# Two double PSUM banks for row maxima and three single banks, in the steps with little filler work

## The chip, the cores and the metric

The kernel runs on one core of one Trainium2 chip. The metric is the device time of one execution in microseconds (us), lower is better. A core has a matrix engine (TensorE, PE in the profile), a vector engine (VectorE, DVE), a scalar engine for functions (ScalarE, ACT), a programmable engine (GpSimd, POOL) and a queue engine for DMAs (SyncE, SP). Matmul results land in PSUM, which has eight banks of 512 fp32 numbers for each of the 128 partitions.

## The reference

Two layers, each an attention block with 16 query heads that share one key and one value head, and a gated feed-forward block; both add to the residual.

```python
def _A_ref(x, wq, wk, wv, wo):
    B, S, D = x.shape          # 1, 2048, 448
    H = 16                     # Dh = 28
    q = (x @ wq).reshape(B, S, H, Dh).transpose(0, 2, 1, 3)
    k = x @ wk
    v = x @ wv
    scores = jnp.einsum("bhqd,bkd->bhqk", q, k) * (Dh ** -0.5)
    p = _softmax(scores, axis=-1)
    o = jnp.einsum("bhqk,bkd->bhqd", p, v)
    return o.transpose(0, 2, 1, 3).reshape(B, S, H * Dh) @ wo

def _B_ref(x, w_gate, w_up, w_down):            # F = 1792
    h = _sigmoid(x @ w_gate) * (x @ w_up)
    return h @ w_down

x = x + _A_ref(_layernorm(x), A_wq, A_wk, A_wv, A_wo)
x = x + _B_ref(_layernorm(x), B_w_gate, B_w_up, B_w_down)
# and both once more, with the same weights
```

## The kernel before

Weights and activations are split into two fp16 parts (high and low), and products are sums of several fp16 matmuls. Queries are worked on in 16 tiles u of 128 rows, keys in 16 tiles kt of 128. The heads form four groups g of four heads each; a group of scores is one matmul of 512 columns.

The main loop (the body of the function behind the start-up) runs over **steps**, one for each (u, kt), 256 in a layer. A step computes:

- four **scores** tiles (`scores`, matmul at L566): keys against the four heads of a group, 128 x 512 in PSUM, named `s`; ScalarE turns each into P = exp(...) in SBUF (L570);
- **PV** (`pv`, L584): four groups of P times the values, added up over the 16 key tiles in one PSUM bank of its own, named `pv`, from pool `psv`;
- two half groups of **maxima** for the next query tile (`mx_gen`, matmul at L509): queries against 512 keys, for two heads at a time, into two PSUM tiles named `mx`; VectorE takes the maximum of each over its 512 columns (L512). They are needed before the scores of that query tile, since the maximum is subtracted inside the score matmul: `maxima` reduces them, transposes them on TensorE (`mt`) and a DMA puts them into the query tile QS;
- **filler** work from `Filler`: generators that give out one matmul at a time, of the query projections of this layer (`qproj`, tile `qp`, 11 matmuls), of the output projection (`wo`, 12 matmuls), and of the feed-forward block (`gp`, `up`, `dn`, matmuls at L369 and L789). `fill.slice` gives out as many as a budget allows (`debt`); `rate` is what is left over the steps that are left.

The order inside two steps is one of two strings, letter by letter: S is a scores tile, M a whole group of maxima (four tiles), m half of one (two tiles), P a PV, T the transposes of finished maxima, F a slice of filler, X the bookkeeping of a step (with stages of the block behind the attention, and in layer 0 pieces of weight preparation, `paced`). `FULL` is used when `rate` is over `LEANR` = 600 and `LEAN` otherwise, which is so at the beginning of each layer, while no feed-forward block is ready:

```python
FULL = "FSFSFSFSTPPXMFSFSFSFSFXM"
LEAN = "FSFSFSFSmPTXmFSFSFSFSmPTXm"
```

At the key tiles of `MORE` = (5, 10) of a layer's first query tile, an additional whole group of maxima is issued.

All engines run their own instructions in order. A PSUM tile is taken from a pool when it is written first and goes back when its last reader is done; the next tile that gets its bank waits for that reader by a semaphore. All tiles but `pv` share one pool `psf` with seven banks, whatever their kind:

```python
BANKS = {"s": "f", "m": "f"}
NBK = {"f": 7, "s": 2, "m": 3}
psf = ctx.enter_context(tc.tile_pool(name="psf", bufs=1, space=PSUM))
```

What reads a PSUM tile is often put off with `defer` and issued at the next `flush`, which a slice of filler begins with.

Of the kernel before, what the change touches and what calls it, by code (L numbers as in the profile page):

```python
# [19 lines left out]
def interleaved_layers_kernel(ctx: ExitStack, tc: tile.TileContext, x, wq, wk, wv, wo, wg, wu, wd, out, layers=2):  # L20
# [27 lines left out]
    psv = ctx.enter_context(tc.tile_pool(name="psv", bufs=1, space=PSUM))  # L48
    BANKS = {"s": "f", "m": "f"}
    NBK = {"f": 7, "s": 2, "m": 3}  # L50
    psf = ctx.enter_context(tc.tile_pool(name="psf", bufs=1, space=PSUM))

# [43 lines left out]
    def fps(shape, dt, name):  # L96
        flush()
        return psf.tile(shape, dt, tag="f", name=name, bufs=NBK["f"])

# [289 lines left out]
    def kv_t(l, XT, t, kt):  # L389
        p = fps([128, 160], F32, "kv")  # L390
        X = lambda c, k: XT[:k, c, t * 128:(t + 1) * 128]
        yield from chain(p[:, 0:128], lambda a, c, k: WKV[:k, a, c, Dh:], X, 64, True)
        yield from chain(p[:, 128:156], lambda a, c, k: WKV[:k, a, c, 0:Dh], X, 40, False)
        c = slice(kt * 128, (kt + 1) * 128)

        def build():
            nc.scalar.activation(KK[l][:, 1, c], p[:, 0:128], AF.Identity, scale=ek, bias=row)
            nc.scalar.activation(VV[l][:, kt, 0:28], p[:, 128:156], AF.Copy, scale=2.0 ** -16)
            nc.vector.scalar_tensor_tensor(KK[l][64:96, 0, c], p[64:96, 0:128], ek[64:96], KK[l][64:96, 1, c],
                                           op0=OP.mult, op1=OP.subtract)  # L400
            nc.gpsimd.tensor_copy(KK[l][0:64, 0, c], KK[l][0:64, 1, c])
        defer(build)

    def kv(l, XT, t, kt):
# [3 lines left out]

        def build():
            nc.scalar.activation(kt_[:, :, 0:28], p[:, None, 28:56].to_broadcast([128, 8, 28]), AF.Copy, scale=ek)  # L410
            nc.scalar.activation(VV[l][:, kt, 0:28], p[:, 0:28], AF.Copy, scale=2.0 ** -16)
# [9 lines left out]
    def qproj(l, XT, b, g):  # L421
# [4 lines left out]

        def ev():
            q = wk1.tile([128, 2, 512], F16, name="qst")
            hi = QH0[:, g] if l + b == 0 else q[:, 0]
# [62 lines left out]
    def mx_gen(l):  # L492
# [3 lines left out]
        for u in range(U):  # L496
# [3 lines left out]
            for kb in range(NB):  # L500
                ks = slice(kb * 512, (kb + 1) * 512 - 128 * (few and kb == NB - 1))
                nk = ks.stop - ks.start
                for g in range(G):
                    assert KVD[l] >= ks.stop // 128
                    for hh in (0, 2):
                        ps = {h: psf.tile([128, 512], F32, tag=BANKS["m"], name="mx", bufs=NBK[BANKS["m"]])
                              for h in (hh, hh + 1)}
                        for h in ps:
                            nc.tensor.matmul(ps[h][:, :nk], qh[32 * h:32 * h + 32, g], KK[l][32 * h:32 * h + 32, 1, ks],  # L509
                                             start=True, stop=True, tile_position=(32 * h, 0))  # L510
                        for h in ps:
                            nc.vector.tensor_reduce(mp[:, g, h, kb:kb + 1], ps[h][:, :nk], axis=AX.X, op=OP.max)  # L512
                        ps = None
                        if hh == 0:
# [8 lines left out]
            if few:  # L523
                assert KVD[l] == KT
                for hh in (0, 2):
                    ps = {h: psf.tile([128, 4, 128], F32, tag=BANKS["m"], name="mx", bufs=NBK[BANKS["m"]])
                          for h in (hh, hh + 1)}
                    for g in range(G):
# [34 lines left out]
    def scores(l, u, kt, g, P):  # L563
        assert ("m", l, u) in stored, (l, u, kt)
        s = psf.tile([128, 512], F32, tag=BANKS["s"], name="s", bufs=NBK[BANKS["s"]])
        nc.tensor.matmul(s, KK[l][0:96, 0, kt * 128:(kt + 1) * 128], QS[l, u][:, g].rearrange("p h n -> p (h n)"),  # L566
# [59 lines left out]
    class Block:  # L626
# [8 lines left out]
        def tile(self, u):  # L635
# [56 lines left out]
            def wo():  # L692
# [7 lines left out]

                def f():
                    nc.vector.scalar_tensor_tensor(self.x1[:, t], p, osc, v["xr"], op0=OP.mult, op1=OP.add)
                    v["ls"] = ln_stats(self.x1[:, t])[0]
# [34 lines left out]
        def bulk(self):  # L738
# [3 lines left out]
            def glu(f):  # L742
# [8 lines left out]
                th = wk1.tile([128, 512], F32, tag="s2", name="th", bufs=3)  # L751
                defer(lambda: nc.scalar.activation(th, gp.rearrange("p j n -> p (j n)"), AF.Tanh, scale=gsc))  # L752
                up = fps([128, 2, TB * 128], F32, "up")
# [3 lines left out]

                def ev():
                    t = th
                    nc.vector.scalar_tensor_tensor(t, th, 1.0, up.rearrange("p j n -> p (j n)"), op0=OP.add, op1=OP.mult)  # L760
# [18 lines left out]
        def down(self, t, hs):  # L779
# [14 lines left out]

            def ev():
                x2 = v["x2"] = wk1.tile([128, D], F32, tag="xr", name="x2", bufs=4)
                nc.vector.scalar_tensor_tensor(x2, p, dsc, self.x1[:, t], op0=OP.mult, op1=OP.add)  # L797
# [43 lines left out]
    class Filler:  # L841
# [16 lines left out]
        def slice(self, ns):  # L858
# [18 lines left out]
            if not self.gens and not self.first:  # L877
                self.debt = min(self.debt, 0.0)

    fill = Filler()  # L880
    LOADS = [(4, 4), (8, 4), (12, 2), (14, 2)]
# [32 lines left out]
    def warmth(n):  # L914
        p = psf.tile([128, 128], F32, tag="f", name="sca", bufs=NBK["f"])
        for _ in range(n):
# [217 lines left out]
    for n in range(NPR):  # L1134
        task("A", 0.9, [], wprep, late=LP, at=PR0 + PRP * n)
    run_tasks(task("V", 0.1, prev[-1:], finish, late=-5.0))
    if not ro:
        load_ro()
# [15 lines left out]
    for l in range(layers):  # L1154
# [12 lines left out]
        if l == 0:  # L1167
            warmth(8)
        rate = 0.0
        PQ = []  # L1170
        step = 0
        P = []
        sn = 0
        while step < U * KT:
            order = FULL if rate > LEANR else LEAN
            for o in order:
                u, kt = divmod(step, KT)
# [83 lines left out]
```

## Time and profile before

| what | us |
| --- | --- |
| median of three runs | 2255.53 (2253.49 to 2256.1) |
| the profiled execution | 2254.95 |
| its span, first to last instruction | 2253.2 |
| ScalarE busy (L570 alone) | 1392.8 (1136.8) |
| POOL busy | 1047.2 |
| lean steps of layer 0, from their first exponential to the first of the step behind them | 107.67 to 265.42 |
| first 44 steps of layer 1, from their first score to the first of the step behind them | 1212.17 to 1349.32 |

The page of a profile lists for each engine its busy time, share of the span and number of instructions; then groups of instructions by source line, engine, operation and tiles (out<-in), with shapes, count, busy time and the mean of one in ns, and behind the second bar the idle time of the engine just before them and who ended it. The order-of-time view lists start, length, engine, line and tiles, merges equal neighbours (x4), and has in brackets the idle time ahead and its releaser. PE rows are matmuls and overlap: a matmul of 512 columns is shown with 0.38 us, though the next one starts 0.22 us behind it. The rows by window give, for a stretch, its length, the busy time and number of instructions of PE, PE's weight loads, DVE, ACT and POOL, then the granted clock, the DMA share and GB/s.

### The profile page before, as it was taken

The numbers are of one execution on the slowest core, as the hardware profiler recorded it, in microseconds if no ns is written. First come the engines' busy times: TensorE is split into PE (matmuls) and PEld (weight loads), VectorE is DVE, ScalarE is ACT, GpSimd is POOL, SyncE is SP. The second block draws the span as 40 slices with busy tenths as digits, with TensorE's granted clock in tenths as the row PEclk, the third lists the DMA queues.
The fourth block names the chain that finished last, engine by engine and source line by source line (L and its number), as shares of the span: only waits on it lengthen the run. The fifth ranks groups of instructions, "written<-read, shape, count | busy, mean of one in ns | idle before, by whom it ended". The sixth has DMA issues, their size and how long they took to land. (4 is left out here: it accounts for less than half of the span.)

```text
span 2253.2 us, 43077 instructions
## 1 busy us (share of the span) xinstructions
PE 2202.5 (98%) x16336; PEld 1059.4 (47%) x16336; DVE 1675.4 (74%) x2921; ACT 1392.8 (62%) x2567; POOL 1047.2 (46%) x1363
## 2 busy tenths in 40 slices
PE   8999999999999999999999999999999999999999
PEld 6322354544545444454573224545454544445457
DVE  7898887877778787774457988878787877878322
ACT  4676766666666666666424676666666666666641
POOL 4367551555455554546402014545545555454540
PEclk8999999999999999999999999999999999999999
DMA  5734642323313232332351113223132313233233
GB/s 150 214 104 134 189 157 61 94 76 103 109 57 105 66 90 80 98 96 79 102 143 57 34 47 107 81 85 101 60 94 65 102 57 102 80 95 89 76 103 122
DMA packets 224400, 217.53 MB, mean 97 GB/s; under 512 B 154048, under 2 KB 185536, under 8 KB 224192
## 3 DMA queue, kind: packets, MB, share of 16 engines
q1 hardware_dynamic: 217200, 198.89, 30.3%
q0 software_dynamic: 3680, 12.09, 1.5%
q10 hardware_dynamic: 3312, 3.79, 0.5%
q8 instruction: 128, 2.10, 0.4%
q14 instruction: 80, 0.66, 0.1%
HBM read 175.37 MB, written 23.59 MB: 88 GB/s over the span
## 5 line engine op out<-in xcount | busy, mean ns | idle before, releaser
L512 DVE TENSOR_REDUCE mp<-mx 128x1 f32<-128x512 f32 x2048 | 1268.0, 680 | 293.7 <-PE mx L509 288.2
L570 ACT ACTIVATE P<-s 128x512 f32<-128x512 f32 x2048 | 1136.8, 600 | 561.9 <-PE s L566 542.7
L566 PE MATMUL s<-QS,KK 96*128 96x512 f16 x2048 | 727.2, 380 | 17.6 <-DVE mp L512 8.3
L369 PEld LDWEIGHTS <-wgu 128*128 128x128 f16 x4928 | 460.4, 97 | 254.9 <-issue 91.8
L604 POOL TENSOR_TENSOR PH<-P,PH 128x512 f16<-128x512 f32 x384 | 459.1, 1195 | 30.8
L603 POOL CAST PH<-P 128x512 f16<-128x512 f32 x384 | 249.4, 649 | 466.6 <-ACT P L570 466.6
L584 PE MATMUL pv<-P,VV 128*32 128x512 f32 x3328 | 418.3, 599 | 0.0
L369 PE MATMUL gp<-XT,wgu 128*128 128x256 f16 x2464 | 387.4, 273 | 0.8 <-DVE mp L512 0.7
L369 PE MATMUL up<-XT,wgu 128*128 128x256 f16 x2464 | 385.7, 273 | 1.0 <-ACT P L570 0.4
L789 PE MATMUL dn<-WD,h 128*128 128x448 f16 x1344 | 330.4, 353 | 0.0
L509 PE MATMUL mx<-KK,QH 32*128 32x512 f16 x2048 | 261.8, 384 | 6.5 <-ACT P L570 3.1
L566 PEld LDWEIGHTS <-KK 96*128 96x128 f16 x2048 | 192.1, 97 | 132.3 <-issue 41.1
L509 PEld LDWEIGHTS <-QH 32*128 32x128 f16 x2048 | 63.8, 91 | 345.1 <-issue 343.1
L789 PEld LDWEIGHTS <-h 128*128 128x128 f16 x1344 | 124.7, 98 | 138.6 <-issue 23.7
L584 PEld LDWEIGHTS pv<-P,VV 128*32 128x32 f32 x3328 | 86.4, 109 | 155.5 <-issue 135.4
L764 DVE SCALAR_TENSOR_TENSOR h<-th,h 128x512 f16<-128x512 f32 x112 | 100.1, 894 | 48.4 <-ACT h L763 48.4
L763 ACT ACTIVATE h<-th 128x512 f16<-128x512 f32 x112 | 70.3, 628 | 87.1 <-DVE th L760 86.1
L760 DVE SCALAR_TENSOR_TENSOR th<-th,up 128x512 f32<-128x512 f32 x112 | 75.9, 678 | 57.3 <-PE up L369 51.8
L675 POOL TENSOR_TENSOR lb<-pvs,lb 128x512 f32<-128x512 f32 x32 | 40.7, 1273 | 141.1 <-DMA lb<-sums 99.3
L752 ACT ACTIVATE th<-gp,gsc 128x512 f32<-128x512 f32 x112 | 76.9, 686 | 44.5 <-PE gp L369 44.1
L369 PE MATMUL qp<-XT,WQ 128*128 128x512 f16 x352 | 100.2, 392 | 0.7 <-DVE ktl L412 0.7
L329 POOL TENSOR_SCALAR rs<-mv 128x1 f32<-128x1 f32 x48 | 11.0, 229 | 179.9 <-DVE mv L324 179.9
(164 smaller groups left out, 1106.9 us busy)
## 6 DMA issues: line engine op xcount, KB each, us to landing
wgu<-wgu_d SPq DMA_DIRECT2D x224, 512.0 KB
QS<-qd SPq DMA_DIRECT2D x384, 32.0 KB
lb<-sums SPq DMA_DIRECT2D x120, 64.0 KB
wgu_d<-sgu POOLq DMA_DIRECT2D x14, 512.0 KB, 3.6
qd<-qst POOLq DMA_DIRECT2D x16, 256.0 KB, 2.6
xr<-in_A_x_dram SPq DMA_DIRECT2D x16, 224.0 KB
QH<-qd SPq DMA_DIRECT2D x28, 128.0 KB
x2d<-x SPq DMA_DIRECT2D x16, 224.0 KB
```

The lines of the kernel that those rows point to most:

```text
L369: nc.tensor.matmul(ps, a, b, start=n == 0, stop=n == 10)
L509: nc.tensor.matmul(ps[h][:, :nk], qh[32 * h:32 * h + 32, g], KK[l][32 * h:32 * h + 32, 1, ks], start=True, stop=True, tile_position=(32 * ...
L512: nc.vector.tensor_reduce(mp[:, g, h, kb:kb + 1], ps[h][:, :nk], axis=AX.X, op=OP.max)
L566: nc.tensor.matmul(s, KK[l][0:96, 0, kt * 128:(kt + 1) * 128], QS[l, u][:, g].rearrange("p h n -> p (h n)"), start=True, stop=True)
L570: nc.scalar.activation(p, s, AF.Exp, scale=ESC)
L584: nc.tensor.matmul(v[32 * g:32 * g + 32], VV[l][:, kt], P[g], start=kt == 0, stop=kt == KT - 1, tile_position=(0, 32 * g))
L603: {"A": nc.scalar.copy, "V": nc.vector.tensor_copy, "P": nc.gpsimd.tensor_copy}[e](h[:, 0], p)
L604: nc.gpsimd.tensor_tensor(h[:, 1], p, h[:, 0], op=OP.subtract)
L752: defer(lambda: nc.scalar.activation(th, gp.rearrange("p j n -> p (j n)"), AF.Tanh, scale=gsc))
L760: nc.vector.scalar_tensor_tensor(t, th, 1.0, up.rearrange("p j n -> p (j n)"), op0=OP.add, op1=OP.mult)
L764: defer(lambda: nc.vector.scalar_tensor_tensor(h[:, 1], t, 2.0 ** -17, h[:, 0], op0=OP.mult, op1=OP.subtract), 1)
L789: nc.tensor.matmul(p, hs[f // 2][:, a, o:o + 128], WD[:, f, c], start=n == 0, stop=n == 3 * FC - 1)
```

## The change

The pool of the seven banks gets two layouts. In layout "F" it is as before. In layout "L" two double banks (tag `m2`, a tile of 2 x 512) belong to the maxima, and three single banks to everything else. A pair of maxima then is one tile, written by the same two matmuls and read by one VectorE instruction over 2 x 512 that gives two numbers a partition. `bank` replaces the direct calls of the pool, and counts the tiles of filler that are open in `live`; the instructions that read them count down (`freed`). Before the layout changes, `Filler.close` runs filler until none is open.

```diff
-    BANKS = {"s": "f", "m": "f"}
-    NBK = {"f": 7, "s": 2, "m": 3}
-    psf = ctx.enter_context(tc.tile_pool(name="psf", bufs=1, space=PSUM))
+    NBK = {"F": 7, "L": 3}
+    pools, psum, live = ctx.enter_context(ExitStack()), {}, [0]
...
+    def banks_as(mode):
+        pools.close()
+        psum["mode"] = mode
+        psum["pool"] = pools.enter_context(tc.tile_pool(name="psf", bufs=1, space=PSUM))
+
+    def bank(shape, dt, name):
+        live[0] += name in ("kv", "qp", "wo", "gp", "up", "dn")
+        return psum["pool"].tile(shape, dt, tag="f", name=name, bufs=NBK[psum["mode"]])
...
-                        ps = {h: psf.tile([128, 512], F32, tag=BANKS["m"], name="mx", bufs=NBK[BANKS["m"]])
-                              for h in (hh, hh + 1)}
+                        two = psum["mode"] == "L"
+                        if two:
+                            both = psum["pool"].tile([128, 2, 512], F32, tag="m2", name="mx", bufs=2)
+                            ps = {h: both[:, h - hh] for h in (hh, hh + 1)}
+                        else:
+                            ps = {h: bank([128, 512], F32, "mx") for h in (hh, hh + 1)}
...
-                        for h in ps:
-                            nc.vector.tensor_reduce(mp[:, g, h, kb:kb + 1], ps[h][:, :nk], axis=AX.X, op=OP.max)
-                        ps = None
+                        if two:
+                            nc.vector.tensor_reduce(mp[:, g, hh:hh + 2, kb:kb + 1], both[:, :, :nk], axis=AX.X, op=OP.max)
+                        else:
+                            for h in ps:
+                                nc.vector.tensor_reduce(mp[:, g, h, kb:kb + 1], ps[h][:, :nk], axis=AX.X, op=OP.max)
+                        ps = both = None
...
-        s = psf.tile([128, 512], F32, tag=BANKS["s"], name="s", bufs=NBK[BANKS["s"]])
+        s = bank([128, 512], F32, "s")
...
+        def close(self):
+
+            flush(True)
+            while live[0]:
+                for q in (self.first, [g[0] for g in self.gens]):
+                    if q:
+                        c = next(q[0], None)
+                        if c is None:
+                            if q is self.first:
+                                q.pop(0)
+                            else:
+                                self.gens.pop(0)
+                        else:
+                            self.debt -= c
+                        break
+                flush(True)
...
         rate = 0.0
+        if psum["mode"] != "L":
+            fill.close()
+            banks_as("L")
...
         while step < U * KT:
             order = FULL if rate > LEANR else LEAN
+            if order is FULL and psum["mode"] == "L":
+                fill.close()
+                banks_as("F")
```

Layout "L" holds from the first step of a layer to the first step with the order FULL: 50 steps in layer 0 and 44 in layer 1, with 104 and 92 reductions of 2 x 512. When a projection ends, the next one of the same generator opens its bank at once, so that `close` only finds nothing open when the generator is done. In layer 0 nothing is open at either change. In layer 1 the change to "L" runs 20 qp matmuls out, and the change back 14. The debt of these then keeps filler away: the next qp matmul comes in the 20th step; four steps follow in the order LEAN with the layout "F", and FULL begins for good with the 50th step (before: the 46th).

Three places show it. On VectorE, in layer 0, a stretch of about ten steps before:

```order
L512 TENSOR_REDUCE mp<-mx 128x1 x10
L144 SCALAR_TENSOR_TENSOR sgu<-rgu,swb,sgu 128x512
L512 TENSOR_REDUCE mp<-mx 128x1 x14
L658 RECIPROCAL rc<-rc 128x16
L512 TENSOR_REDUCE mp<-mx 128x1 x4
L594 TENSOR_TENSOR VH<-VV,VH 128x256
```

and the same stretch of the change:

```order
L533 TENSOR_REDUCE mp<-mx 128x2 x5
L158 SCALAR_TENSOR_TENSOR sgu<-rgu,swb,sgu 128x512
L533 TENSOR_REDUCE mp<-mx 128x2 x7
L681 RECIPROCAL rc<-rc 128x16
L533 TENSOR_REDUCE mp<-mx 128x2 x2
L617 TENSOR_TENSOR VH<-VV,VH 128x256
```

Each two reductions have become one, and nothing has changed places around them. On TensorE, a step of the lean part of layer 0 before, with the engine whose semaphore a matmul waits for (weight loads left out), and the pair of maxima behind it:

```order
L566 MATMUL s_2141<-QS_1721,KK_130 128x512 [waits Activation_49]
L566 MATMUL s_2145<-QS_1721,KK_130 128x512 [waits DVE_49]
L566 MATMUL s_2149<-QS_1721,KK_130 128x512 [waits Activation_49]
L566 MATMUL s_2153<-QS_1721,KK_130 128x512 [waits DVE_49]
L509 MATMUL mx_2157<-KK_130,QH0_139 128x512 [waits DVE_49]
L509 MATMUL mx_2158<-KK_130,QH0_139 128x512 [waits Activation_49]
```

and the same step of the change, with the pair of maxima behind it:

```order
L589 MATMUL s_2107<-QS_1697,KK_130 128x512 [waits Activation_49]
L589 MATMUL s_2111<-QS_1697,KK_130 128x512 [waits Activation_49]
L589 MATMUL s_2115<-QS_1697,KK_130 128x512 [waits Activation_49]
L589 MATMUL s_2119<-QS_1697,KK_130 128x512 [waits Activation_49]
L530 MATMUL mx_2123<-KK_130,QH0_139 128x512 [waits DVE_49]
```

The order of the matmuls is the same. Two of the four scores had got banks that maxima had left, and now all four get banks that scores have left, with three in the ring. The third place is TensorE's begin of layer 1, before (weight loads left out; qp are query projections, and "..." stands for more matmuls of the same tile):

```order
L369 MATMUL qp_16710<-XT1_12374,WQ_100 128x512
...
L369 MATMUL qp_16744<-XT1_12374,WQ_100 128x512
...
L566 MATMUL s_16749<-QS_15845,KK_1462 128x512
L566 MATMUL s_16753<-QS_15845,KK_1462 128x512
L566 MATMUL s_16757<-QS_15845,KK_1462 128x512
L566 MATMUL s_16761<-QS_15845,KK_1462 128x512
```

and in the change:

```order
L383 MATMUL qp_16510<-XT1_12174,WQ_100 128x512
...
L383 MATMUL qp_16544<-XT1_12174,WQ_100 128x512
...
L383 MATMUL qp_16560<-XT1_12174,WQ_100 128x512
...
L589 MATMUL s_16582<-QS_15645,KK_1462 128x512
L589 MATMUL s_16586<-QS_15645,KK_1462 128x512
L589 MATMUL s_16590<-QS_15645,KK_1462 128x512
L589 MATMUL s_16594<-QS_15645,KK_1462 128x512
```

Tile qp_16744 had two of its 11 matmuls ahead of the first score; its namesake qp_16544 has all 11 there, and a third projection, qp_16560, its 11 as well. On SP's queue two loads of feed-forward weights (wgu) stand later by some places, and on POOL's two stores of projections (qd); nothing else is moved.

More of the change, by code (lines that the diff above doesn't have):

```diff
@@ L48, in interleaved_layers_kernel, with freed @@
     psv = ctx.enter_context(tc.tile_pool(name="psv", bufs=1, space=PSUM))
-    BANKS = {"s": "f", "m": "f"}
-    NBK = {"f": 7, "s": 2, "m": 3}
-    psf = ctx.enter_context(tc.tile_pool(name="psf", bufs=1, space=PSUM))
+    NBK = {"F": 7, "L": 3}
+    pools, psum, live = ctx.enter_context(ExitStack()), {}, [0]
+    def freed():
+        live[0] -= 1
+    def banks_as(mode):
[5 more added lines that the diff above has]
+        return psum["pool"].tile(shape, dt, tag="f", name=name, bufs=NBK[psum["mode"]])
+    START = "F"
+    banks_as(START)
     jp = big.tile([128, 128], I32, tag="big", name="jp")
@@ L97, in fps @@
         flush()
-        return psf.tile(shape, dt, tag="f", name=name, bufs=NBK["f"])
+        return bank(shape, dt, name)
     C512, C448, C256, C128, C32 = 216, 190, 110, 56, 110
@@ L396, in build @@
         def build():
+            freed()
             nc.scalar.activation(KK[l][:, 1, c], p[:, 0:128], AF.Identity, scale=ek, bias=row)
@@ L409, in build @@
         def build():
+            freed()
             nc.scalar.activation(kt_[:, :, 0:28], p[:, None, 28:56].to_broadcast([128, 8, 28]), AF.Copy, scale=ek)
@@ L427, in ev @@
         def ev():
+            freed()
             q = wk1.tile([128, 2, 512], F16, name="qst")
@@ L525, in mx_gen @@
                 for hh in (0, 2):
-                    ps = {h: psf.tile([128, 4, 128], F32, tag=BANKS["m"], name="mx", bufs=NBK[BANKS["m"]])
-                          for h in (hh, hh + 1)}
+                    ps = {h: bank([128, 4, 128], F32, "mx") for h in (hh, hh + 1)}
                     for g in range(G):
@@ L701, in f @@
                 def f():
+                    freed()
                     nc.vector.scalar_tensor_tensor(self.x1[:, t], p, osc, v["xr"], op0=OP.mult, op1=OP.add)
@@ L751, in glu @@
                 th = wk1.tile([128, 512], F32, tag="s2", name="th", bufs=3)
-                defer(lambda: nc.scalar.activation(th, gp.rearrange("p j n -> p (j n)"), AF.Tanh, scale=gsc))
+                defer(lambda: freed() or nc.scalar.activation(th, gp.rearrange("p j n -> p (j n)"), AF.Tanh, scale=gsc))
                 up = fps([128, 2, TB * 128], F32, "up")
@@ L758, in ev @@
                 def ev():
+                    freed()
                     t = th
@@ L795, in ev @@
             def ev():
+                freed()
                 x2 = v["x2"] = wk1.tile([128, D], F32, tag="xr", name="x2", bufs=4)
@@ L914, in warmth @@
     def warmth(n):
-        p = psf.tile([128, 128], F32, tag="f", name="sca", bufs=NBK["f"])
+        p = bank([128, 128], F32, "sca")
         for _ in range(n):
@@ L1136, in interleaved_layers_kernel @@
     run_tasks(task("V", 0.1, prev[-1:], finish, late=-5.0))
+    live[0] = 0
     if not ro:
```

## The prediction

> **What bounds the kernel now.** I read the page first, then the busy times of the two stretches that the change can reach, then the order of time inside single steps of these. The page puts TensorE first and VectorE second, and the costliest group of VectorE is the one that the change rewrites.
>
> ```profile
> PE 2202.5 (98%) x16336; PEld 1059.4 (47%) x16336; DVE 1675.4 (74%) x2921; ACT 1392.8 (62%) x2567; POOL 1047.2 (46%) x1363
> L512 DVE TENSOR_REDUCE mp<-mx 128x1 f32<-128x512 f32 x2048 | 1268.0, 680 | 293.7 <-PE mx L509 288.2
> ```
>
> Only the lean steps change their banks: the first 50 steps of layer 0 (stage A) and the first 44 of layer 1 (stage B). These rows give their ends (first exponential of stage A and of the step behind it, first score matmul of stage B and of the step behind it), and their busy times (share of PE, PEld, DVE, ACT, POOL).
>
> ```profile
> 107.67 2.08 ACT L570 ACTIVATE P<-s 128x512 f32<-128x512 f32 x4
> 265.42 1.11 ACT L570 ACTIVATE P<-s 128x512 f32<-128x512 f32 x2
> 1212.17 1.04 PE L566 MATMUL s<-QS,KK 96*128 96x512 f16 x4 [0.35 <-DVE mp L512]
> 1349.32 1.04 PE L566 MATMUL s<-QS,KK 96*128 96x512 f16 x4
> 107.70:265.40 157.70, 147.16 (x836) 37.96 (x839) 145.69 (x257) 116.31 (x228) 113.59 (x101) 0.99 0.44 134
> 1212.20:1349.30 137.10, 135.10 (x781) 36.86 (x781) 124.26 (x208) 95.91 (x186) 10.60 (x21) 1.00 0.15 40
> ```
>
> Stage A takes 157.75 us, 3.15 a step; stage B 137.15, 3.12 a step. VectorE is busy 92% and 91% of them, TensorE 93% and 99%. So both are near their limit, and which one a change relieves or burdens must be read from a step. This is a step of stage A without a wait:
>
> ```profile
> 223.25 0.39 PE L509 MATMUL mx<-KK,QH 32*128 32x512 f16 x2
> 223.57 1.04 PE L566 MATMUL s<-QS,KK 96*128 96x512 f16 x4
> 224.00 2.06 ACT L570 ACTIVATE P<-s 128x512 f32<-128x512 f32 x4 [0.65 <-PE s L566]
> 224.65 0.39 PE L509 MATMUL mx<-KK,QH 32*128 32x512 f16 x2
> 224.97 1.07 PE L584 MATMUL pv<-P,VV 128*32 128x512 f32 x8
> 225.97 0.39 PE L509 MATMUL mx<-KK,QH 32*128 32x512 f16 x2
> 226.29 1.04 PE L566 MATMUL s<-QS,KK 96*128 96x512 f16 x4
> ```
>
> From score matmul to score matmul 226.29 - 223.57 = 2.72 us: scores 1.08, a pair of maxima 0.32, PV 1.00, a pair 0.32. The four scores leave TensorE within a microsecond, while ScalarE needs 2.06 us for them: the difference stands in PSUM. In stage B the same step carries about one qp matmul more (0.22 us).
>
> **What the change saves.** 196 pairs of one-bank reductions become 196 reductions of two banks. The trace has reductions in a row at two widths:
>
> ```profile
> 130.85 7.25 DVE L512 TENSOR_REDUCE mp<-mx 128x1 f32<-128x512 f32 x12
> 1197.06 5.69 DVE L512 TENSOR_REDUCE mp<-mx 128x1 f32<-128x384 f32 x12
> L512 DVE TENSOR_REDUCE mp<-mx 128x1 f32<-128x384 f32 x16 | 7.6, 549 | 0.1
> ```
>
> Start to start they stand (7.25 - 0.68) / 11 = 0.597 us and (5.69 - 0.55) / 11 = 0.467 us apart, so an element costs 0.130 / 128 = 1.02 ns and an instruction 0.077 us beside its elements. A reduction of 1024 elements is not in the trace: by these two it takes 1.12 us of VectorE instead of 1.19, and 196 x 0.077 = 15.1 us is what VectorE gets back. At worst a read across two banks saves nothing (0); at best the difference of whole durations, 680 + 512 x 1.03 against 2 x 680, is 0.15 us each, 29 us. I take 15.1. It shortens the run only where VectorE ends a step.
>
> [...]
>
> **What it costs: banks.** Maxima now own four banks, the accumulator one, so three are left for scores and everything else; before, seven were shared. A step has four scores. The fourth can start only when the first of its own step has been read, in every lean step. The trace of before has this case, since its ring sometimes deals the banks so:
>
> ```profile
> 132.88 0.39 PE L509 MATMUL mx<-KK,QH 32*128 32x512 f16 x2
> 133.21 0.82 PE L566 MATMUL s<-QS,KK 96*128 96x512 f16 x3
> 133.63 2.07 ACT L570 ACTIVATE P<-s 128x512 f32<-128x512 f32 x4 [1.15 <-PE s L566]
> 134.28 0.38 PE L566 MATMUL s<-QS,KK 96*128 96x512 f16 x1 [0.25 <-ACT P L570]
> 134.59 0.55 PE L509 MATMUL mx<-KK,QH 32*128 32x512 f16 x2
> 135.07 1.06 PE L584 MATMUL pv<-P,VV 128*32 128x512 f32 x8
> 136.06 0.39 PE L509 MATMUL mx<-KK,QH 32*128 32x512 f16 x2
> 136.38 0.39 PE L566 MATMUL s<-QS,KK 96*128 96x512 f16 x1
> ```
>
> The fourth score starts 1.07 us behind the first, named as waiting for ScalarE's P, and the step takes 136.38 - 133.21 = 3.17 us. Of that 0.16 is the second maximum's wait (0.48 from mx to pv where the free step has 0.32), which the wide pairs make less likely. So a step with **three** score banks costs 1.07 + 0.31 + 0.32 + 1.00 + 0.32 = 3.02 us, with 3.17 as the upper bound. Behind the waiting score on TensorE's queue stand the pair of maxima and PV, so nothing else runs meanwhile.
>
> A query projection (qp) holds a bank from its first matmul until VectorE has read it. In the built program one is open from the 20th step of stage B to its end, 25 steps, so the scores have **two** banks there. The third score then waits for the first exponential (at 1.07), the fourth for the second. ScalarE starts 0.42 behind the first score and goes on every (2.07 - 0.60) / 3 = 0.49, so the second ends at 0.42 + 0.49 + 0.60 = 1.51, the fourth score starts at about 1.57, and the step is 1.57 + 0.31 + 0.32 + 1.00 + 0.32 = 3.52 us. The qp matmuls between scores then fit into these waits and cost nothing. No row shows such a step; it lies between 3.02 (no second bank missed) and 3.68 (with the 0.16 again).
>
> Terms that both stages share come from these rows: the wo burst on TensorE, and its reader on VectorE, who frees the bank; and in stage A ScalarE waiting for POOL.
>
> ```profile
> 1341.75 2.44 PE L697 MATMUL wo<-WO,oT 128*128 128x448 f16 x12
> 1344.03 1.03 PE L566 MATMUL s<-QS,KK 96*128 96x512 f16 x4
> 1344.23 0.68 DVE L702 SCALAR_TENSOR_TENSOR x<-wo,osc,xr 128x448 f32<-128x448 f32 x1 [1.10 <-PE wo L697]
> 184.07 0.62 ACT L681 CAST oT<-lb 128x512 f16<-128x512 f32 x1 [3.57 <-POOL lb L675]
> L570 ACT ACTIVATE P<-s 128x512 f32<-128x512 f32 x200 | 103.3, 605 | 35.3 <-PE s L566 35.0
> ```
>
> A wo burst is 1344.03 - 1341.75 = 2.28 us, and its bank is free only at 1344.91, so a score behind it waits some 0.5 more.
>
> Stage A, step by step of the sum: 50 x 3.02 = 151.0; two wo bursts 5.6; four extra pairs of maxima (at the key tiles of MORE) 4 x 0.32 = 1.3; three transposes of maxima 1.5; ScalarE held up behind POOL 2.5 (of the 3.57, since longer steps give POOL's chain more time); ScalarE's other work in the way of an exponential, 5 of its 116.3 - 103.3 = 13.0 (seven banks let scores run ahead of it, three don't); VectorE's crowded steps 1.5. Together 168.4, that is **+10.7**. With VectorE's 104 x 0.077 = 8.0 fully felt it could be about 0, with 3.17 a step +18.
>
> Stage B. Ahead of it, closing the filler runs the open projections out: 20 qp matmuls move ahead of the first score. They take
>
> ```profile
> 1195.79 1.90 PE L369 MATMUL qp<-XT,WQ 128*128 128x512 f16 x8
> 1211.59 0.69 ACT L430 ACTIVATE qst<-qp,eq 128x512 f16<-128x512 f32 x1 [2.13 <-DMA qd<-qst]
> ```
>
> (1.90 - 0.38) / 7 = 0.217 us each, 4.3 us; the 0.35 of the first score's wait covers part (3.8 left), and ScalarE's evictions, which wait for the DMAs of qst, stand ahead of the first exponential, 0.5: 4.3. Then 19 x 3.02 = 57.4; the extra pairs and a transpose 2.1; 25 x 3.52 = 88.0; two wo bursts 5.6; steps in which qp changes banks or leads the step 3.2; and 14 qp matmuls run out at the end, 3.0 + 0.5. Together 164.1. Behind the stage 13 qp matmuls are gone from the steps up to the 50th, -2.8: 161.3 against 137.15, **+24.1**. Lowest, with the two-bank steps at 3.02 and no extra waits, about +8; highest, with 0.16 in each of the 44 steps, +31.
>
> Moved with the projections are their DMAs on POOL's queue (qd<-qst) and two weight loads on SP's; POOL is busy 10.6 us of stage B, so I give them nothing. Everything else has the banks it had and is bound by TensorE: no change. The sum is 10.7 + 24.1 = 34.8 us on the profiled execution's 2254.95, **2290 us**; the median of the runs is 0.6 higher, which is inside their spread.
>
> **The rivals.** (1) Faster: VectorE is the bound of these steps, TensorE's waits for banks are slack, and the saved 15.1 us come off: 2240. For it speak 92% and 91% busy. Against it: VectorE waits for maxima rather than the other way round in stage B (8.8 us idle below, PE's mx idle of 0.7), and the 3.02 of TensorE alone exceeds four reductions at 2.24 a step. It decides wherever VectorE's work in a step is over 3.02 (3.52 with two banks), that is with over 0.78 us of other work. Chance 0.08.
>
> ```profile
> L512 DVE TENSOR_REDUCE mp<-mx 128x1 f32<-128x512 f32 x183 | 115.3, 682 | 8.8 <-PE mx L509 7.9
> L509 PE MATMUL mx<-KK,QH 32*128 32x512 f16 x184 | 37.9, 382 | 0.7 <-DVE mp L512 0.2
> ```
>
> (2) Only stage B pays, because in stage A, with its preparation work, VectorE's 8.0 us offset the waits: 2255 + 24.1 = 2279. Chance 0.15. (3) The change's wide reductions don't save (a read over two banks costs like two) and the second pair of double banks comes late as well: 0.16 in nearly every step, 18 + 31 = 49 more, 2304. Chance 0.10. (4) No net change: gains and waits cancel, 2255, chance 0.04; TensorE's 135.1 of 137.1 us busy leaves no room to hide 24 us in stage B.
>
> **How the numbers follow.** The forecast has 0.63. The range goes from 2263 (stage A at 0, stage B at its lowest) to 2308 (both at their highest, and a little of ScalarE's queue on top); cases (1) and (4) are left out. A measurement of this kernel tells about 0.2% from no change. Faster 0.08, same 0.04, slower 0.88.
>
> **What would show it.** In the profile after, lean steps of stage A should repeat every 3.0 us with the fourth score 1.07 behind the first and waiting for ScalarE, the last 25 of stage B every 3.5 with two waits; the wide reduction should last about 1.2 us, and VectorE's busy time fall by some 15 to 30 us while its idle time before mx grows. Twenty qp matmuls in a row should stand ahead of the first score of layer 1. I am wrong if lean steps stay at 2.7 to 2.8 us, if scores don't wait for P, or if stages behind the lean ones change by more than a few microseconds.

## The result, and the profile after

The changed kernel takes 2312.74 us (median of 4 executions, 2304.04 to 2318.21) against 2254.6 us before (4, 2253.49 to 2256.1): ratio 1.0257, 95% interval 1.0235 to 1.0279. It is slower by 2.6%. The forecast was 2290 with a range up to 2308: the sign and the waits for banks came out as forecast, but the move was 58 us instead of 35. The profiled execution took 2318.21 us (span 2316.4); it is the slowest of the four, so its stages show more than the median does.

On the page of the change, the busy rows, the row of the granted clock (in 40 slices, 9 is full speed) and three groups of instructions answer to those of before:

```profile
PE 2232.2 (96%) x16336; PEld 1057.9 (46%) x16336; DVE 1671.0 (72%) x2725; ACT 1395.4 (60%) x2567; POOL 1044.8 (45%) x1363
...
PEclk9979999999999999999999998999999999999999
...
L536 DVE TENSOR_REDUCE mp<-mx 128x1 f32<-128x512 f32 x1656 | 1024.4, 680 | 294.5 <-PE mx L530 290.7
L589 PE MATMUL s<-QS,KK 96*128 96x512 f16 x2048 | 746.1, 386 | 50.6 <-ACT P L593 31.3
...
L533 DVE TENSOR_REDUCE mp<-mx 128x2 f32<-128x1024 f32 x196 | 238.0, 1224 | 66.5 <-PE mx L530 61.0
```

The row of the scores before was:

```profile
L566 PE MATMUL s<-QS,KK 96*128 96x512 f16 x2048 | 727.2, 380 | 17.6 <-DVE mp L512 8.3
```

The 196 wide reductions are there, and scores now wait 31.3 us for ScalarE's P, where before all idle time ahead of them was 17.6 us. VectorE has 196 instructions less, but its busy time fell by 4.4 us only (1675.4 before). TensorE does the same 16336 matmuls and is busy 30 us longer: the same work ran slower somewhere.

This is a lean step of stage A on TensorE, in order of time, from score matmul to score matmul:

```profile
217.72 0.82 PE L589 MATMUL s<-QS,KK 96*128 96x512 f16 x3
218.80 0.38 PE L589 MATMUL s<-QS,KK 96*128 96x512 f16 x1 [0.25 <-ACT P L593]
219.11 0.39 PE L530 MATMUL mx<-KK,QH 32*128 32x512 f16 x2
219.42 1.06 PE L607 MATMUL pv<-P,VV 128*32 128x512 f32 x8
220.42 0.39 PE L530 MATMUL mx<-KK,QH 32*128 32x512 f16 x2
220.74 0.39 PE L589 MATMUL s<-QS,KK 96*128 96x512 f16 x1
```

The fourth score starts 218.80 - 217.72 = 1.08 us behind the first, waiting for P, and the step takes 220.74 - 217.72 = 3.02 us, as forecast. With a query projection open, so with two banks for scores, a step of stage B is:

```profile
1346.83 0.60 PE L589 MATMUL s<-QS,KK 96*128 96x512 f16 x2
1347.91 0.86 PE L589 MATMUL s<-QS,KK 96*128 96x512 f16 x2 [0.47 <-ACT P L593]
1348.70 0.39 PE L530 MATMUL mx<-KK,QH 32*128 32x512 f16 x2
1349.02 1.07 PE L607 MATMUL pv<-P,VV 128*32 128x512 f32 x8
1350.02 0.39 PE L530 MATMUL mx<-KK,QH 32*128 32x512 f16 x2
1350.34 0.39 PE L589 MATMUL s<-QS,KK 96*128 96x512 f16 x1
```

That is 1350.34 - 1346.83 = 3.51 us, where 3.52 was forecast. Not forecast is the price of a step in which `MORE` adds a group of maxima (VectorE's row between the two of TensorE):

```profile
1255.76 0.82 PE L589 MATMUL s<-QS,KK 96*128 96x512 f16 x3
...
1258.46 0.79 PE L530 MATMUL mx<-KK,QH 32*128 32x512 f16 x4
...
1257.57 7.27 DVE L533 TENSOR_REDUCE mp<-mx 128x2 f32<-128x1024 f32 x6 [0.48 <-PE mx L530]
...
1260.17 0.39 PE L530 MATMUL mx<-KK,QH 32*128 32x512 f16 x2 [0.92 <-DVE mp L533]
1260.49 0.82 PE L589 MATMUL s<-QS,KK 96*128 96x512 f16 x3
```

Two double banks hold two pairs, so the third pair waits until VectorE is through with the first. The step goes from 1255.76 to 1260.49, 4.73 us, where the prediction had 3.02 + 2 x 0.32 = 3.66. The rows by window of three stages, and a table of all stages, show where the rest is (columns as before; the granted clock is the number behind POOL's count):

```profile
104.60:284.60 180.00, 157.98 (x832) 37.56 (x831) 143.48 (x153) 116.87 (x228) 112.00 (x99) 0.91 0.39 120
...
1239.00:1403.70 164.70, 145.52 (x775) 36.28 (x774) 121.96 (x117) 98.33 (x185) 11.11 (x23) 0.96 0.10 28
1403.70:1427.40 23.70, 22.80 (x94) 4.72 (x93) 14.71 (x26) 12.86 (x25) 7.61 (x9) 0.64 0.09 22
```

| stage | before, us | after, us | difference | granted clock after |
| --- | --- | --- | --- | --- |
| stage A, 50 lean steps of layer 0 | 157.7 | 180.0 | +22.3 | 0.91 |
| rest of layer 0 | 828.7 | 829.7 | +1.0 | 1.00 |
| last step of layer 0 to layer 1's first | 118.5 | 124.7 | +6.2 | 0.99 |
| stage B, 44 lean steps of layer 1 | 137.1 | 164.7 | +27.6 | 0.96 |
| the next six steps | 19.1 | 23.7 | +4.6 | 0.64 |
| the rest | 884.3 | 888.9 | +4.6 | 1.00 |

The start-up ahead of stage A was 3.1 us shorter in the change's profile, so the differences add up to 63.2 us of span. In before's trace the same stages had a clock of 0.99 or 1.00. So two things are in the result beside the moved work: waits for banks, and a clock of TensorE that fell. The clock of half speed comes in whole stretches. Two of them, each with the 3.4 us ahead of it:

```profile
105.60:109.00 3.40, 1.74 (x9) 0.71 (x10) 2.28 (x9) 1.54 (x5) 0.00 (x0) 1.00 0.38 91
109.00:139.70 30.70, 29.25 (x102) 5.50 (x102) 19.98 (x27) 16.12 (x33) 4.62 (x4) 0.50 0.21 57
...
1235.40:1238.80 3.40, 1.33 (x7) 0.53 (x6) 0.96 (x2) 0.69 (x1) 0.72 (x1) 1.00 0.69 217
1238.80:1249.00 10.20, 10.20 (x38) 1.90 (x36) 5.90 (x5) 6.19 (x12) 0.72 (x1) 0.50 0.12 37
```

The wait in the first of these windows, 1.54 us ahead of small matmuls in layer 0's first step, is not new. The profile before has it too, and the clock held at 1.00 behind it:

```profile
109.67 0.35 PE L128 MATMUL sca<-mxb,one 128*128 128x2 f32 x2 [1.55 <-DVE mxb L254]
```

In a stretch at half speed a lean step takes 122.64 - 117.88 = 4.76 us, without a wait, because its matmuls take nearly twice as long (the eight rows of PV span 1.94 us here, and 1.06 in the first step above):

```profile
117.88 1.89 PE L589 MATMUL s<-QS,KK 96*128 96x512 f16 x4
119.70 0.61 PE L530 MATMUL mx<-KK,QH 32*128 32x512 f16 x2
120.24 1.94 PE L607 MATMUL pv<-P,VV 128*32 128x512 f32 x8
122.10 0.60 PE L530 MATMUL mx<-KK,QH 32*128 32x512 f16 x2
122.64 1.03 PE L589 MATMUL s<-QS,KK 96*128 96x512 f16 x2
```

### The profile page after: what moved, and what is told of

Same layout as the page of the kernel before. It is cut to its first block, busy times and chain, and to the rows that moved or that the text cites. A ratio compares the mean times of both kernels' runs of the same rounds, so it can differ in the third digit from the quotient of the medians.

```text
span 2316.4 us, 42731 instructions
## 1 busy us (share of the span) xinstructions
PE 2232.2 (96%) x16336; PEld 1057.9 (46%) x16336; DVE 1671.0 (72%) x2725; ACT 1395.4 (60%) x2567; POOL 1044.8 (45%) x1363
## 5 line engine op out<-in xcount | busy, mean ns | idle before, releaser
L536 DVE TENSOR_REDUCE mp<-mx 128x1 f32<-128x512 f32 x1656 | 1024.4, 680 | 294.5 <-PE mx L530 290.7
L589 PE MATMUL s<-QS,KK 96*128 96x512 f16 x2048 | 746.1, 386 | 50.6 <-ACT P L593 31.3
L607 PE MATMUL pv<-P,VV 128*32 128x512 f32 x3328 | 428.5, 612 | 0.0
L533 DVE TENSOR_REDUCE mp<-mx 128x2 f32<-128x1024 f32 x196 | 238.0, 1224 | 66.5 <-PE mx L530 61.0
L814 PEld LDWEIGHTS <-h 128*128 128x128 f16 x1344 | 124.7, 98 | 139.3 <-issue 24.6
```

Source lines behind the costliest of these rows:

```text
L533: nc.vector.tensor_reduce(mp[:, g, hh:hh + 2, kb:kb + 1], both[:, :, :nk], axis=AX.X, op=OP.max)
L607: nc.tensor.matmul(v[32 * g:32 * g + 32], VV[l][:, kt], P[g], start=kt == 0, stop=kt == KT - 1, tile_position=(0, 32 * g))
L814: nc.tensor.matmul(p, hs[f // 2][:, a, o:o + 128], WD[:, f, c], start=n == 0, stop=n == 3 * FC - 1)
```

## The experiments

Each kernel ran beside the one before on the same chip; ratios are to that. The last column is the mean granted clock of the timed executions, as a median; before has 0.994.

| kernel | median, us | ratio, 95% interval | clock |
| --- | --- | --- | --- |
| the change | 2312.74 | 1.0257 (1.0235 to 1.0279) | 0.987 |
| single banks for maxima | 2315.32 | 1.0261 (1.0223 to 1.03) | 0.986 |
| layer 0 alone | 2271.93 | 1.0067 (1.0045 to 1.0089) | 0.992 |
| layer 1 alone | 2294.04 | 1.0162 (1.0145 to 1.018) | 0.990 |
| maxima between the scores | 2294.05 | 1.0157 (1.014 to 1.0174) | 0.987 |
| before, in that order | 2266.62 | 1.0054 (1.0037 to 1.0071) | 0.993 |
| third score twice | 2309.24 | 1.0228 (1.0196 to 1.0261) | 0.990 |
| closing alone | 2269.87 | 1.0067 (1.0049 to 1.0085) | 0.992 |
| one double bank | 2345.07 | 1.0391 (1.0368 to 1.0414) | 0.980 |
| dummy matmuls behind closings | 2313.24 | 1.0256 (1.0236 to 1.0275) | 0.991 |
| second and third score twice | 2317.08 | 1.0263 (1.0235 to 1.029) | 0.988 |
| the change again | 2313.37 | 1.0262 (1.0234 to 1.0291) | 0.987 |
| gaps filled | 2304.66 | 1.0204 (1.0183 to 1.0224) | 0.993 |

**Is it the pairs or the banks?** The maxima keep their four banks, as singles with a reduction each.

```diff
-                            both = psum["pool"].tile([128, 2, 512], F32, tag="m2", name="mx", bufs=2)
-                            ps = {h: both[:, h - hh] for h in (hh, hh + 1)}
+                            ps = {h: psum["pool"].tile([128, 512], F32, tag="m1", name="mx", bufs=4) for h in (hh, hh + 1)}
...
-                            nc.vector.tensor_reduce(mp[:, g, hh:hh + 2, kb:kb + 1], both[:, :, :nk], axis=AX.X, op=OP.max)
+                        for h in ps:
+                            nc.vector.tensor_reduce(mp[:, g, h, kb:kb + 1], ps[h][:, :nk], axis=AX.X, op=OP.max)
```

> The change with its four maxima banks as four single banks, and one reduction for each again; the three banks of the scores, the closing of the filler and the new layouts stay. Theory (score banks): the time is lost by scores that wait for one of three or two banks, and by the TensorE clock that falls in these stretches; then it stays at 2300 to 2320 us, lean steps at 3.02 and 3.51 us, although VectorE has some 15 us more to do. Rival (the pair): the double bank and its one long reduction hold TensorE up; then more than half of the loss goes, 2285 us or less.

2315.32 us, the same as the change. The wide reduction is worth nothing here, and the loss doesn't come from it.

**Which layer pays?**

```diff
-        if psum["mode"] != "L":
+        if psum["mode"] != "L" and l == 0:
```

> The change with its lean layout in layer 0 alone; layer 1 keeps seven banks throughout. Theory (score banks and clock): layer 0's lean steps took 22 us more in the profile, so 2277 us, between 2264 and 2285, with lean steps at 3.02 us and at about 4.76 where the clock is at half. Rival (closing the filler costs): nothing is run out in layer 0, so the time is within 5 us of before, 2250 to 2260.

> The change with its lean layout in layer 1 alone. Theory (score banks): 28 us in the 44 steps, 6 ahead of them and 5 behind, so 2293 us, between 2285 and 2300, and with the kernel of layer 0 alone it adds up to the change within 8 us. Rival (closing): the loss is the same, but it stands ahead of the first score and at the change back, not in the steps.

Layer 0 alone costs 2271.93 - 2255.45 = 16.5 us, layer 1 alone (`l == 1`) 38.6, together 55 of the change's 58. So both stages pay, and rival (2) falls. In the profile of layer 0 alone, stage A lost little clock:

```profile
106.40:276.80 170.40, 147.86 (x832) 36.67 (x831) 142.79 (x153) 116.95 (x227) 113.79 (x100) 0.98 0.42 129
```

170.4 us is +12.6, where the sum had +10.7. The difference of 9.6 us to the change's 180.0 is the clock: 34.1 us of stage A were at half speed there and 8.4 us here, and 25.7 x (1 - 3.02 / 4.76) = 9.4.

**Does the wait go if the maxima stand between the scores?** Then two scores follow each other instead of four. The same order was also given to the kernel before.

```diff
-    LEAN = "FSFSFSFSmPTXmFSFSFSFSmPTXm"
+    LEAN = "FSFSmPFSFSTXmFSFSmPFSFSTXm"
```

> The change with another order of a lean step: a pair of maxima and PV stand between the second and the third score, not behind the fourth. Theory (score banks): the third and the fourth score then come 1.3 us later and find their banks read, with three banks and with two; lean steps fall to 2.6 to 2.8 us, the clock holds, and what is left is the closing of the filler: 2265 us, between 2250 and 2275. Rival (the pair): nothing changes, 2300 us or more.

> The kernel before, seven shared banks, with the lean order that has a pair of maxima and PV between the second and the third score. Theory (score banks): there is little to win where seven banks are shared, the lean steps stay at 2.6 to 2.8 us and the time within 0.5% of before, 2245 to 2265; then the gain of this order in the changed kernel came from its three banks. Rival (the order is better by itself): 20 us or more faster than before, as it was in the changed kernel.

TensorE in the change with this order, where the clock is full:

```profile
194.95 0.61 PE L589 MATMUL s<-QS,KK 96*128 96x512 f16 x2
195.49 0.39 PE L530 MATMUL mx<-KK,QH 32*128 32x512 f16 x2
195.81 1.06 PE L607 MATMUL pv<-P,VV 128*32 128x512 f32 x8
196.81 0.60 PE L589 MATMUL s<-QS,KK 96*128 96x512 f16 x2
```

The wait for P is gone, and stage B took 153.2 us in this profile instead of 164.7. The time fell to 2294.05, not to what was expected. Two things are seen to stand in the way: the order itself costs the kernel before 2266.62 - 2253.52 = 13 us, and the clock stayed at 0.987, with stage A at 177.7 us. Against before in the same order the layout still costs some 27 us, clock included.

**What does closing cost by itself?** The layout "L" gets seven shared banks, so that only the closing and the later begin of FULL are left.

```diff
-    NBK = {"F": 7, "L": 3}
+    NBK = {"F": 7, "L": 7}
...
-                        two = psum["mode"] == "L"
+                        two = False
```

> The change with its lean layout set to seven shared single banks and single reductions: closing the filler, changing the layout and the order that follows remain, bank split and wide reduction are gone. Theory (score banks): what remains is 3 us ahead of layer 1, 1 to 5 us at the change back and 4 to 5 us in the steps behind it, less the qp matmuls that left the lean steps: 2262 us, between 2255 and 2270. Rival (closing costs most of it): 2280 us or more.

16 us (2269.87 against 2253.52), at the upper end of what was expected. Rows by window, from the last step of layer 0 to layer 1, stage B, the next six steps, and the rest:

```profile
1096.90:1219.60 122.70, 116.06 (x889) 73.61 (x887) 74.70 (x136) 28.57 (x51) 24.39 (x53) 1.00 0.43 125
1219.60:1356.00 136.40, 132.73 (x775) 36.61 (x774) 124.71 (x209) 96.09 (x185) 11.15 (x23) 1.00 0.12 33
1356.00:1376.00 20.00, 18.80 (x95) 4.36 (x94) 14.76 (x26) 12.82 (x26) 7.58 (x9) 0.83 0.11 28
1376.00:2264.80 888.80, 880.11 (x6755) 452.06 (x6753) 611.23 (x1012) 537.28 (x963) 425.94 (x540) 1.00 0.29 89
```

The projections that are run out cost 4.2 us ahead of stage B, as forecast (4.3). But the six steps behind it, which have 95 matmuls instead of 124, are no shorter (20.0 against 19.1, at a clock of 0.83), and the rest is 4.5 us longer. At full clock, which the kernel with dummy matmuls behind the closings had there, the six steps take 17.75 us, so 29 or 30 matmuls fewer are worth some 1.3 us. The longer rest (by 4 to 6 us) stands in every kernel that closes in layer 1, and in none that doesn't (884.5 us in the kernel with layer 0 alone). It is work that moved there: the rest has 6755 matmuls instead of 6740, and 21 of the feed-forward block (gp), which before stand in the six steps, now come behind them. Of the 4.5 us, 4.4 lie in its twenty steps from the 61st to the 80th of the layer, before and with closing alone:

```profile
1407.50:1486.50 79.00, 78.99 (x599) 37.70 (x598) 63.18 (x106) 51.29 (x92) 41.22 (x51) 1.00 0.26 78
1414.40:1497.80 83.40, 82.45 (x625) 40.21 (x623) 63.05 (x106) 51.56 (x92) 40.55 (x50) 1.00 0.28 85
```

TensorE has hardly any idle time to give there. Filler has left steps that become hardly shorter without it, and has come into steps that become longer by it.

**More banks for the scores instead.** One double bank, five singles.

```diff
-    NBK = {"F": 7, "L": 3}
+    NBK = {"F": 7, "L": 5}
...
-                            both = psum["pool"].tile([128, 2, 512], F32, tag="m2", name="mx", bufs=2)
+                            both = psum["pool"].tile([128, 2, 512], F32, tag="m2", name="mx", bufs=1)
```

> The change with one double bank for the maxima and five single banks for everything else. Theory (score banks): scores and a projection find banks now, so their waits go; but each pair of maxima waits for the reduction of the pair ahead, some 0.3 us twice a step, so lean steps of about 3.3 us in layer 0 and in layer 1 alike: 2290 us, between 2275 and 2305. Rival (not the scores' banks): as the change or slower, 2305 us or more.

```profile
190.75 1.04 PE L589 MATMUL s<-QS,KK 96*128 96x512 f16 x4
192.14 0.39 PE L530 MATMUL mx<-KK,QH 32*128 32x512 f16 x2 [0.35 <-DVE mp L533]
...
193.85 0.39 PE L530 MATMUL mx<-KK,QH 32*128 32x512 f16 x2 [0.32 <-DVE mp L533]
```

The scores no longer wait, and now the maxima do, at each pair. The step takes 3.42 us, from 190.75 to the next score at 194.17, about as expected. But in a step with additional maxima each pair more waits 1.3 us, and the clock was 0.980: it is the slowest of all, 2345.07.

**What brings the clock down?** First theory: the 0.25 us that TensorE waits in each lean step. Score matmuls were issued twice into the same bank, for the third score, then for the second and third.

```diff
+        if psum["mode"] == "L" and g in (1, 2):
+            nc.tensor.matmul(s, KK[l][0:96, 0, kt * 128:(kt + 1) * 128], QS[l, u][:, g].rearrange("p h n -> p (h n)"),
+                             start=True, stop=True)
```

> The change, with the third score matmul of each lean step issued twice into its bank (the same result), so that 0.2 us of TensorE's wait for the fourth score's bank is filled with matmul work. Lean steps with three banks should stay at 3.02 us. Theory (the idle in every step lets the granted clock fall): the half-speed time in the lean steps shrinks by more than half, mean clock 0.990 or more in every run, and the time falls to 2298 to 2305 us. Rival (single gaps, or chance): the clock stays as in the change, 0.983 to 0.991, and the time at 2305 to 2320.

> The change, with the second and the third score matmul of each lean step issued twice, so that TensorE has no wait of 0.25 us ahead of the fourth any more (two extra matmuls, 0.43 us; the fourth score would start 5 x 0.217 = 1.09 behind the first instead of 1.07, so steps stay at 3.02 to 3.05, and 3.5 with two banks). Theory (the lean steps run at half clock because TensorE works too little in them): half-clock time falls to 30 to 45, clock to .994 or more, time 2297 to 2302. Rival (the gaps ahead of the stages, or something without relation to how much TensorE works): half-clock time as in the change, 50 to 80, time 2312 to 2316.

With both, the step (L592 is the repeated matmul) has no wait ahead of the fourth score:

```profile
186.93 0.61 PE L589 MATMUL s<-QS,KK 96*128 96x512 f16 x2
187.37 0.38 PE L592 MATMUL s<-QS,KK 96*128 96x512 f16 x1
187.59 0.38 PE L589 MATMUL s<-QS,KK 96*128 96x512 f16 x1
187.81 0.38 PE L592 MATMUL s<-QS,KK 96*128 96x512 f16 x1
188.02 0.38 PE L589 MATMUL s<-QS,KK 96*128 96x512 f16 x1
```

Yet the clock stayed at 0.988 and the time at 2317.08. The steady waits aren't the main cause. A small share is not excluded by these two kernels: three of their ten executions had a clock of 0.993 to 0.996, and the ten of the change 0.978 to 0.991. Second theory: the longer gaps. The change with 16 small matmuls on a constant behind every closing (`warmth(16)`), and the change itself again beside it:

> The change, with 16 small fp32 matmuls on a constant (2.05 us for 16 in the change's trace) behind each closing, so that TensorE works through the gap behind it (2.07 us before layer 1's first lean step, 1.56 us before its first step in layout F; in layer 0 nothing is waited for there, so they cost about 2 us at each of its two places). Theory (a gap of 1.5 to 2 us behind a closing is what starts the stretches at half clock): half-clock time falls from 79 us to 35 to 50 and the mean granted clock rises to .992 or more, so the time is 2312 - 13 + 4 = about 2303, fast runs 2298. Rival (the gaps don't matter, the lean steps themselves do): half-clock time stays at 60 to 80, time 2312 to 2318.

> The change itself once more, for the spread of its granted clock beside the two others: median 2312 (2304 to 2318), clock .983 to .991, if its clock is drawn anew in each execution; if the clock goes with the chip, all executions within 0.2% of each other.

No gain: 2313.24 us, though the time at half speed fell from 79 to 41 us in the profile, as expected. The 16 matmuls took 3.7 us, not the 2.05 expected (an fp32 matmul stands as two rows in the trace, PV's four as eight and these 16 as 32, and 16 rows had been taken for 16 matmuls), which ate what the clock gave (0.991 against 0.987). But the place moved. In layer 1 of its profile the clock no longer fell at the first step; it fell behind the two steps with additional maxima, the second of them here:

```profile
1271.50:1274.90 3.40, 2.22 (x14) 0.59 (x10) 3.31 (x4) 0.73 (x3) 0.00 (x0) 1.00 0.00 0
1274.90:1288.60 13.70, 13.70 (x48) 2.50 (x48) 8.12 (x10) 5.58 (x12) 0.00 (x0) 0.50 0.00 1
```

The change again shows how much of this is chance: one program on one chip took 2306.56 to 2328.64 us, at clocks of 0.990 to 0.978. So the last kernel fills all three kinds of gaps: small matmuls behind layer 1's closings and in layer 0's first step, and the additional maxima as single pairs in four steps instead of two pairs in two.

```diff
-    MORE = (5, 10)
+    MORE = (3, 5, 8, 10)
...
-                        group(mx)
+                        next(mx, None)
...
+            if l:
+                warmth(16)
             banks_as("L")
...
+                if l:
+                    warmth(16)
                 banks_as("F")
...
+                        if step == 0:
+                            warmth(12)
```

> The change with its three kinds of gaps filled that stand ahead of a stretch at half clock in the traces so far: 16 small matmuls on a constant behind layer 1's two closings (in the change TensorE is busy 1.33 us of the 3.4 us ahead of 1238.8, where the clock falls), 12 ahead of the sums that wait 1.54 us in layer 0's first step (1.74 us busy of the 3.4 ahead of 109.0), and the extra maxima spread over four steps as one pair each instead of two steps with two pairs (2.22 busy of the 3.4 ahead of 1257.9 and of 1274.9 in the run with small matmuls behind the closings). Theory (the clock falls behind a window of about 3.4 us in which TensorE was busy only half to two thirds, and what makes such windows are these gaps, not the 0.25 us that each lean step waits): no stretch at half clock starts at these places, the sum falls from 79 us to 25 to 45 us, what is left stands where the transposes, the output projection and the first steps of layout F are, clock .992 or more, time 2298 to 2306. Rival (the lean steps themselves bring the clock down, wherever they are): stretches move to other lean steps, the sum stays at 55 to 80, clock .985 to .991, time 2308 to 2316.

2304.66 us, clocks 0.992 to 0.998, half speed for 38 us of the profile against 79 in the change. Stage B and the six steps behind it:

```profile
1232.50:1392.80 160.30, 143.60 (x807) 39.34 (x806) 121.25 (x117) 98.17 (x185) 11.12 (x22) 1.00 0.11 30
1392.80:1415.40 22.60, 21.44 (x94) 4.64 (x93) 14.73 (x26) 12.87 (x25) 6.89 (x8) 0.70 0.06 11
```

Stage B ran at full clock throughout, with the same steps of 3.02 and 3.51 us. So in stages A and B the gaps bring the clock down; the lean steps don't, even with their waits. Of the two stretches at half speed that are left from stage A on, one (10.2 us) stands in stage A behind a gap that wasn't filled, 2.16 us of waiting for P, and the other (13.7 us) in the six steps behind stage B. The three fillings came together, so the share of each isn't known. No kernel here beats the one before.

## Why the prediction was right in its direction and short in its size

- **The bank prices were right.** Three banks 3.02 us a step, two banks 3.51 (3.52 forecast), with the waits where they were expected, and twenty matmuls of query projections ahead of layer 1. With little loss of clock (0.98), stage A cost 12.6 us for the forecast's 10.7.
- **VectorE's saving: worth nothing, as the sum had it, but its size was wrong.** Six wide reductions in a row take 7.27 us, (7.27 - 1.22) / 5 = 1.21 each, and two single ones 2 x 0.597 = 1.19. The prediction had 1.12, and VectorE's busy time fell by 4.4 us, where 15 to 30 were to be seen. The first half of rival (3), that a read over two banks costs like two, is what happened. (Fully felt, the saving of 8.0 us would have left 10.7 - 8.0 = 2.7 us of stage A's loss, not the 0 that the low end of the range took.)
- **The additional maxima were mis-sized**: 4.73 us for 3.66, which is 4 x 1.07 = 4.3 us if all four such steps cost the same. The sum counted TensorE's matmuls and left out that two double banks hold two pairs, while a third comes.
- **The closing was mis-sized.** The term of 4.3 us ahead of stage B was right. "Behind the stage 13 qp matmuls are gone from the steps up to the 50th, -2.8" and "Everything else has the banks it had and is bound by TensorE: no change" were wrong: the steps became only some 1.3 us shorter at full clock, and the rest became 4.5 us longer by the matmuls that moved into it. Net +5.0 was forecast.
- **The step that failed most is one that isn't there: the clock.** The sum multiplied steps by durations at full speed (50 x 3.02, 25 x 3.52) and put the clock at nothing, without a reason. The change adds gaps in TensorE's work (2.07 us ahead of stage B's first score, 1.56 us behind the stage, 0.92 us in a step with additional maxima), and at gaps TensorE can fall to half speed for some time: for 79 us of the change's profile, against 24 before.

How much is which? The ten executions of the change lie near one line, 1.8 us for each 0.001 of mean clock; the 36 of before 1.4. Read at before's clock, 0.994 (0.003 beyond the change's best), the change has 2299.6 and before 2255.2: +44.4. The other 13 to 14 us of the median's 58 are clock. The profile agrees: 78.5 - 24.3 = 54 us more at half speed, times 1 - 3.02 / 4.76, are 20 us of its 63, which leaves 43. Closing alone, read in the same way (1.6 us for each 0.001, four executions), has 2265.1, +10; its stages in layer 1, at full clock, add up to 4.2 - 0.7 - 1.3 + 4.5 = 6.7. So at equal clock: closing 7 to 10 (5 forecast), banks 34 to 38 (30 forecast, and the steps with additional maxima would be 4 of what is missing). The split is worked out from such lines, not measured by one kernel.

Rivals (1), VectorE as the bound, and (4), no net change, fall with the result; the single reductions, which leave the time as it was, speak against (1) once more. Rival (2) falls with the layers run apart.

## What to carry to other kernels

Banks split by kind take freedom from the kind with the most tiles in flight: count the tiles of one step against what is left to them, and price the step from the moment the first reader frees a bank; here that was right to 0.01 us. Then ask of every wait whether it is a steady one, as the 0.25 us in each lean step, or a single gap, as those of 0.9 to 2.1 us here: gaps can cost several times their length, through the clock (1.54 us of waiting came with 11 us in the change's stage A, and with none before). Before work is moved to empty a pool, look at whether it was cheap where it stood, and whether there is idle time where it will go.

## What the hardware showed that was not expected

Half clock came in the change's profile in stretches of 3.4, 6.8, 10.2, 17.1 and 30.7 us, 1, 2, 3, 5 and 9 times 3.4. The clock fell behind 3.4 us with TensorE busy 1.33 or 1.74 us there, and 2.22 us with dummy matmuls behind the closings, and it stayed at half for 30.7 us in which TensorE was busy 29.25. Not every such window brought it down, and one stretch of 17 us (from 1409.5 in the change) began behind 3.4 us with 2.87 us busy.

The fourteen profiles can be cut into windows of 3.41 us (30.7 / 9) that start and end with the stretches at half clock. How often half clock followed a window at full clock goes with how long TensorE was busy in it:

| TensorE busy in 3.41 us | windows at full clock | half clock next |
| --- | --- | --- |
| below 2.0 us | 89 | 64 |
| 2.0 to 2.3 us | 63 | 27 |
| 2.3 to 2.7 us | 146 | 11 |
| 2.7 to 3.0 us | 484 | 9 |
| over 3.0 us | 8392 | 0 |

The steady lean steps of stage B with all gaps filled have 2.83 to 3.16 us in such a window. All nine falls of the fourth row stand in the six steps behind stage B, in nine of the eleven kernels that close in layer 1, and no gap like the others stands ahead of them; why the clock falls there is open.

What decides when the clock comes back wasn't tried either. Every stretch ended with a window in which TensorE was busy for at least 3.2 us, but 90 such windows at half clock were followed by another. At the gap in layer 0's first step, the four kernels with seven banks there ran at half speed for 0, 0, 3.4 and 3.4 us, and the nine that split the banks and didn't fill it for 3.4 to 34.1 us. So the steps behind a gap may hold the clock down; no run separates this from chance.

A gap is thus dear by chance: 1.54 us of waiting came with 30.7 x (1 - 3.02 / 4.76) = 11 us in the change's stage A, and with none before.
